# Four places of a written-out order moved: a GELU ahead of a decoding step, a join ahead of K S, a Gram ahead of two transpositions, an output on another queue

## The chip, the cores and the metric

The kernel runs on one core of a Trainium2 chip. A core has five engines, each with a queue of its own that it works through in order: TensorE (PE: matmuls, with the weight loads shown as PEld), VectorE (DVE), ScalarE (ACT), GpSimd (POOL) and SyncE (SP), which here only issues DMAs; ACT issues some too. The metric is the device time of one execution in microseconds; lower is better.

## The reference, cut to what matters

```python
# q, k, v: (4, 8, 768, 48); beta: (4, 8, 768)
k_n = k / (norm(k) + 1e-6)
for t in range(S):                       # delta rule, state of D x D for each batch and head
    y[:, :, t] = q[:, :, t] @ state
    v_old = state.T @ k_n[:, :, t]
    state = state + beta[t] * outer(k_n[:, :, t], v[:, :, t] - v_old)
x = y.transpose(0, 2, 1, 3).reshape(3072, 384)
h = x @ w_in                             # (384, 2048)
out = (0.5 * h * (1 + erf(h / sqrt(2)))) @ w_out      # (2048, 384)
```

q, k, v and beta arrive in float32; w_in and w_out arrive as float64, which the kernel reads as pairs of 32-bit words and turns into float32 itself ("decoding").

## The kernel before, in words

**Tiling.** The 768 steps are cut into 12 chunks of 64. A chunk has two units (`tiles[c, a]`, a = 0, 1), each with two batches on the two halves of the partitions and eight heads. `first`, `third` and `fourth` are the units of chunks 0 and 1, of chunk 2 and of chunk 3.

**Delta rule.** Inside a chunk the steps are solved together. Two chunks (four units) make a group g. The Gram matrices of K (`grams`, matmuls L414 by way of `products`, psum tile psG) give `G` and `diag`. VectorE eliminates the 32-wide diagonal blocks row by row in `Nu` (`eliminate_steps`, L501 and L503, one pair for a row); at the end two transpositions write the inverse to `XM` (L512) and `Zf` (L516). A "join" (`join_run`, L593, tile psJ) then builds the off-diagonal blocks: level 0 needs XM, is scaled into XM by VectorE (L605); level 1 is copied into Zf by ACT (L572). It comes in three calls, join1[0], join1[1] and join1[2], for group 1. For each chunk `against_state` multiplies K and Q with the state ("K S", L667, psK), `subtract` makes W on VectorE (L678, L684) and y on ACT (L679), `solve` gives U (psU, L702), `use` and `update` give the outputs and the state's increment (psY, L732 and L743), `outputs` writes St (L748) and x (L758), and `turn` transposes x into xT (L779, L780).

**Norms.** `norms(c)` squares K of a chunk on ACT (`ksq`), `prep(c)` sums the squares on VectorE (L349) and takes the power on GpSimd (L351), `finish(c)` makes the factors gm for the pair of chunks c and c + 1 on VectorE (L303 to L307), and the first steps of the elimination turn gm into a scaled mask (L476, L477).

**Feed-forward.** Chunks 0 and 1 use plain layers: `fc1` fills psH for a block f of 128 hidden units (three matmuls of 128x256; PE shows six, [...]and a "block" below means these six passes), ACT writes its GELU into `G` (GELU f for short); `fc2` accumulates 16 blocks into psO (L829), which ACT copies to `o_sb` and `send` writes out (L823). psH and psO have two PSUM buffers between them (tag "mlp"). Chunks 2 to 11 use a Strassen-like scheme with fewer products (`part_of_layer`, L916 and `second_layer`, L859). In its first layer a block b makes products named P1, P5, P6, P2, R22, R11, P7, P3, R12, P4, R21, in this order on PE; X1, Z1, Y1 and V1 are its psum tiles, `pu` holds copies of X1 and Z1 (ACT), L939, L968, L947 and L958 are its additions on VectorE. P4 and R21 add to Y1, so P4 must wait until L947 has read it.

**Decoding.** W_in has eight parts n; for each, `begin` isolates the exponents' bits on VectorE (L231), `exponents` turns them into float scales with two ACT instructions, `mantissas` (L251, L253) and `signed` (L261) finish the part. Part n serves blocks 2n and 2n + 1. The raw words are fetched by SP, four parts ahead. The parts of W_out follow in the same manner.

**Order.** The first part of the program is ordered by hand. The rest is a `plan`: a list of (time, step) pairs, made by `at(first, last, steps)`, which are sorted by their time and emitted (`emit`). The times are a scale of the author's, one unit for a chunk's layer, and not microseconds. VectorE runs in the emitted order; on the other engines a scheduler may shift instructions, except that `together` and `behind` chain groups of matmuls on PE, and `keep` keeps ACT instructions in the emitted order. A DMA that `fetch_in`, `load_blocks` or `send` emits stands in the issuing engine's queue and waits there until its buffer is free or its data ready.

Of the kernel before, what the change touches and what calls it, by code (L numbers as in the profile page):

```python
# [19 lines left out]
def kernel(  # L20
# [28 lines left out]
    nc = tc.nc  # L49
# [4 lines left out]
    NC = S // C  # L54
# [48 lines left out]
    for c in range(NC):  # L103
        for a in range(NA):
            u = tiles[c, a] = Unit()
# [171 lines left out]

    def decode_in():

        marks = {3: (None, 1.03, 0.99, 1.04), 4: (1.0, 1.09, 1.1, 1.13),  # L280
                 5: (1.12, 1.18, 1.14, 1.2), 6: (1.19, 1.24, 1.21, 1.25),
                 7: (1.245, 1.3, 1.29, 1.36)}
        steps = []
        for n, (a, b, c, d) in marks.items():
            if a is not None:
                steps += [(a, (begin, n))]
            steps += [(b, (exponents, n, keep)), (c, (mantissas, n)), (d, (signed, n))]
        return steps
# [349 lines left out]
    def join_steps(g):  # L638
        a, b = range(NA), range(NA, 2 * NA)
        return [(join_run, g, a, ()), (join_run, g, b, a), (join_run, g, (), b)]  # L640
# [176 lines left out]
            nc.scalar.activation(*gelu)  # L817

    def send(u, cols=slice(0, DM), queues=None):
        queues = queues or ((nc.sync, nc.sync) if 1 < u.c < NC - 1 else (nc.scalar, nc.scalar))  # L820
        for p in range(2):
            row = (2 * u.a + p) * S + u.c * C
            queues[p].dma_start(out=out[row:row + C, cols], in_=u.o[HALF[p], cols])  # L823

    def fc2(u, f0, f1):
        if f0 == 0:
            u.psO = ps.tile([128, DM], F32, tag="mlp", name="psO")
        for f in range(f0, f1):
            nc.tensor.matmul(u.psO, lhsT=G[:, u.a, f, :],  # L829
                             rhs=w_out_sb[:, f, :], start=(f == 0), stop=(f == NF - 1))  # L830
        if f1 == NF:
            u.o = wk.tile([128, DM], F32, tag="o_sb", name="o_sb")
            nc.scalar.copy(u.o, u.psO)
            send(u)
# [206 lines left out]
    def ffn_steps(c):  # L1041
        ones = [(1.3, fc1, c, f) for f in range(NF)]
        if c > 1:
            return [(0.88, part_of_layer, c, b, n) for b in range(NB)
                    for n in ("P1", "P5", "P6", "P2", "R22", "R11", "P7", "P3", "R12", "P4", "R21")] + [
                (2.6, second_layer, c, n) for n in (1, 5, 2, 6, 4, 7, 3)]
        twos = [(2.7, fc2, tiles[c, a], f, f + 4) for a in range(NA) for f in range(0, NF, 4)]
        if c == 0:
            twos.sort(key=lambda s: s[3])
            more_ = [(1.3, fc1, 1, f) for f in range(EARLY)]  # L1050
            return ones + twos[:-2 * NA] + more_[:4] + twos[-2 * NA:-NA] + more_[4:] + twos[-NA:]
        return ones[EARLY:] + twos

    def at(first, last, steps):

        total, done, timed = sum(s[0] for s in steps), 0.0, []
        for w, *step in steps:
            timed.append((first + (last - first) * (done + 0.5 * w) / total, step))
            done += w
        return timed  # L1060
# [69 lines left out]
    fourth = [tiles[3, a] for a in range(NA)]  # L1130
# [58 lines left out]
    def state_at(c, *times, first=(), second=()):  # L1189

        steps = state_steps(c, first, second)
        if len(times) > len(steps):
            steps = steps[:-1] + [(turn, tiles[c, a]) for a in range(NA)]
        return [(t, step) for t, step in zip(times, steps) if t is not None]

    plan = [at(c + 1 + 0.25 * (c == 1), c + 2 + 0.25 * (c == 0), ffn_steps(c)) for c in range(NC)]
    plan += [decode_in(), at(1.365, 1.9, decode_steps(n_in, NW)), at(1.91, 1.911, [(1.0, late)])]
    rows1, join1 = eliminate_steps(1), join_steps(1)
    plan += [at(1.06, 1.065, [(1.0, load, 3)]),
# [8 lines left out]
             at(1.455, 1.456, [(1.0, solved, first[NA + 1], kept_copy)]),  # L1208
             state_at(1, None, None, 1.5, 1.56, 1.58),
             at(1.92, 2.45, rows1[:-1]),  # L1210
             at(2.66, 2.661, [(1.0, together, join1[0])]),
             at(2.662, 2.663, rows1[-1:]),
             at(2.65, 2.651, [(1.0, sum_of_w_in, 1)]), at(2.664, 2.665, [(1.0, sum_of_w_in, 2)]), at(2.712, 2.713, [(1.0, sum_of_w_in, 4)]),
             at(2.72, 2.721, [(1.0, sum_of_w_in, 3)]),
# [25 lines left out]
    def gram(c):  # L1240
        return [(grams, [tiles[c, a] for a in range(NA)])] if c < NC else []

    def query(c):
        return [(queries, [tiles[c, a] for a in range(NA)])]

    def spread(name, n, *times):
        return [at(t, t + 0.001, [(1.0, copy_out, name, n)]) for t in times]

    def rows_of(g, w, pieces):
        rows = eliminate_steps(g)  # L1250
        assert sum(n for n, _, _ in pieces) == len(rows)
        parts, done = [], 0
        for n, first, last in pieces:
            parts += [at(w + first, w + last, rows[done:done + n])]
            done += n
        return parts
# [8 lines left out]
    for w in range(3, NC):  # L1265
        two_ahead = w + 2 < NC
        if w % 2:
            if w == 3:
                plan += [at(w + 0.09, w + 0.092, [(1.0, transposed, u, (1,)) for u in fourth]
                            + [(1.0, together, *gram(5))]),  # L1270
                         at(w, w + 0.001, [(1.0, norms, 5), (1.0, prep, 5)]),
                         at(w + 0.1, w + 0.101, [(1.0, finish, 4)])]
                plan += rows_of(2, w, ((1, 0.102, 0.103), (2, 0.16, 0.2), (4, 0.224, 0.31),
                                       (2, 0.325, 0.365), (1, 0.395, 0.4), (2, 0.485, 0.5),
                                       (2, 0.508, 0.54), (5, 0.6, 0.685), (7, 0.76, 0.88),
                                       (3, 1.0, 1.05), (5, 1.07, 1.1), (1, 1.153, 1.154),
                                       (1, 1.2, 1.201), (1, 1.201, 1.202)))
            elif two_ahead:
                plan += rows_of(w // 2 + 1, w, ((1, -0.35, -0.349), (1, -0.34, -0.339),
                                                (1, -0.23, -0.229), (5, -0.22, -0.14),  # L1280
                                                (1, -0.07, -0.06), (3, 0.005, 0.05),
                                                (3, 0.068, 0.148), (2, 0.156, 0.215),
                                                (2, 0.235, 0.31), (3, 0.325, 0.365),
                                                (1, 0.398, 0.409), (2, 0.485, 0.5),
                                                (1, 0.508, 0.54), (5, 0.6, 0.685),
                                                (3, 0.76, 0.8), (1, 1.003, 1.004),
                                                (1, 1.16, 1.161), (1, 1.166, 1.167)))
            plan += [state_at(w, w + 0.367, w + 0.59, w + 0.72, w + 0.93, second=query(w))]
        else:
            j0, j1, j2 = join_steps(w // 2)  # L1290
            t = w + (0.25 if w == 4 else 0.165)
            plan += [at(t, t + 0.001, [(1.0, together, j0, *query(w))]),
                     at(w + 0.37, w + 0.371, [(1.0, together, j1, *gram(w + 2))]),
                     state_at(w, w + 0.465, w + 0.58, w + 0.72, w + 0.93, second=[j2] + gram(w + 3))]
            plan += spread("join", 4, w + 0.395)
            plan += spread("join", 4, w + 0.64)
            if two_ahead:
                plan += spread("gram", 2, w + 0.375) + spread("gram", 2, w + 0.42)
                plan += spread("gram", 4, w + 0.63)
                plan += [at(w + 0.366, w + 0.367, [(1.0, norms, w + 2)]), at(w + 0.3715, w + 0.372, [(1.0, prep, w + 2)]),  # L1300
                         at(w + 0.56, w + 0.561, [(1.0, norms, w + 3), (1.0, prep, w + 3)]),
                         at(w + 0.64, w + 0.641, [(1.0, finish, w + 2)])]
# [32 lines left out]
```

## Time and profile before

| | |
|---|---|
| three runs | 643.37, 643.89, 644.04 us; median 643.89 |
| profiled execution | 644.36 us, of which span 642.6 us |
| PE busy | 621.4 us (97%) |
| VectorE, ACT, GpSimd busy | 496.1, 259.7, 63.7 us |
| granted TensorE clock, mean | 0.983 |
| waits of PE in the span | 2.1 us psH on ACT's G, 5.1 us psT on the first K, 3.7 us psG on Qt, 0.6 us psX on pu, 0.5 us psX on x |
| DMA | 39.79 MB, 62 GB/s |

The profile counts microseconds from the span's start. In an order of time a row gives start, length, engine, line, operation, output and inputs, count, and in brackets the idle time of the engine ahead of it with what ended it. Neighbouring rows of one engine overlap a little[...]. A row "SPq" or "ACTq" is the issue of DMAs by that queue.

### The profile page before, as it was taken

To read this page: it belongs to the slowest core of one execution; us is meant where nothing else is said; L and a number is where in the kernel's file an instruction comes from. 1 tells how busy PE (TensorE), PEld (TensorE's weight loads), DVE (VectorE), ACT (ScalarE), POOL (GpSimd) and SP (SyncE) were. 2 spreads that over 40 slices of the span, in tenths; PEclk is the share of its full clock that TensorE was granted. 3 is DMA by queue.
4 is the path that set the end of the run, shared out by engine and by line. 5 is a ranking of instruction groups with operands and counts; after the bars stand their busy time and mean duration, and the time that the engine had idled before them with its cause. 6 is when DMAs were issued, how large, how long until landed. Compare 5 with 4: busy or idle time off the path is not lost.

```text
span 642.6 us, 22154 instructions
## 1 busy us (share of the span) xinstructions
PE 621.4 (97%) x9702; PEld 575.8 (90%) x9702; DVE 496.1 (77%) x1011; ACT 259.7 (40%) x586; POOL 63.7 (10%) x58
## 2 busy tenths in 40 slices
PE   6778999999899999999999999999999999999997
PEld 5667886777699999999999999999999999999997
DVE  6999889988889997999587999587999565354342
ACT  3576776624452266132266132266132253232230
POOL 4044001100401013001013001013001000000000
PEclk9977999999999999999999999999999999999999
DMA  9895764303432335321425312311221400100100
GB/s 130 180 272 159 131 159 148 50 1 67 73 61 37 57 41 89 60 26 35 67 36 83 61 23 40 67 23 31 52 26 34 68 3 3 26 2 3 24 3 24
DMA packets 158433, 39.79 MB, mean 62 GB/s; under 512 B 150016, under 2 KB 153216, under 8 KB 158336
## 3 DMA queue, kind: packets, MB, share of 16 engines
q1 hardware_dynamic: 155344, 36.94, 29.9%
q10 hardware_dynamic: 2992, 1.43, 1.0%
q8 instruction: 76, 1.25, 0.8%
q14 instruction: 21, 0.17, 0.1%
HBM read 33.62 MB, written 4.72 MB: 60 GB/s over the span
## 4 chain that ended last, share of the span: by engine, by line
PE 86%; DVE 6%; ACT 3%; DMA 2%; issue 1%; SPq 1%; DVEq 0%; ACTq 0%
PE psX L859 12%; PE psY L916 11%; PE psX L916 8%; PE psY L859 8%; PE psH L811 6%; PE psV L916 5%; PE psO L829 5%; PE psZ L916 5%; PE psG L414 4%; PE psZ L859 4%; PE psV L859 4%; PE psK L667 3%; PE psJ L593 2%; PE psY L732 2%; PE psU L702 2%; DMA Kp<-in_k_dram 1%
## 5 line engine op out<-in xcount | busy, mean ns | idle before, releaser
L916 PE MATMUL psX<-xT,w_in_sb 128*128 128x128 f32 x480 | 64.6, 278 | 0.6 <-ACT pu L902 0.6
L503 DVE TENSOR_TENSOR Nu<-Nu,tmp 128x58 f32<-128x58 f32 (+13 forms) x168 | 58.9, 351 | 5.8
L501 DVE TENSOR_TENSOR tmp<-Nu 128x58 f32<-128x58 f32 (+13 forms) x168 | 59.0, 351 | 4.4
L916 PEld LDWEIGHTS psX<-xT,w_in_sb 128*128 128x128 f32 x480 | 58.8, 192 | 1.8 <-ACT pu L902 0.8
L902 ACT COPY xT<-psX 128x768 f32<-128x768 f32 x9 | 7.2, 798 | 124.4 <-PE psX L788 124.4
L859 PE MATMUL psX<-w_out_sb,G 128*128 128x192 f32 x320 | 55.3, 326 | 0.0
L351 POOL TENSOR_TENSOR n<-n,half 128x16 f32<-128x16 f32 x10 | 30.0, 2998 | 254.1 <-DVE n L349 194.6
L859 PEld LDWEIGHTS psX<-w_out_sb,G 128*128 128x128 f32 x320 | 52.1, 190 | 0.0
L811 PE MATMUL psH<-xT,w_in_sb 128*128 128x256 f32 x192 | 46.3, 398 | 2.2 <-ACT G L902 2.1
L811 PEld LDWEIGHTS psH<-xT,w_in_sb 128*128 128x128 f32 x192 | 37.4, 199 | 9.7 <-ACT G L902 2.7
L829 PE MATMUL psO<-w_out_sb,G 128*128 128x384 f32 x128 | 44.5, 492 | 0.0
L916 PE MATMUL psY<-xT,w_in_sb 128*128 128x128 f32 x320 | 42.3, 275 | 0.0
L902 ACT COPY pu<-psZ 128x512 f32<-128x512 f32 x40 | 23.4, 586 | 39.0 <-PE psZ L916 38.9
L916 PEld LDWEIGHTS psY<-xT,w_in_sb 128*128 128x128 f32 x320 | 38.9, 192 | 0.0
L829 PEld LDWEIGHTS psO<-w_out_sb,G 128*128 128x128 f32 x128 | 23.5, 190 | 13.6
L902 ACT ACTIVATE G<-G 128x512 f32<-128x512 f32 x40 | 25.2, 629 | 19.0 <-DVE G L947 18.3
L376 POOL TENSOR_TENSOR V<-V,n 128x384 f32<-128x384 f32 x18 | 16.2, 910 | 133.5 <-DMA V<-in_v_dram 78.4
L859 PE MATMUL psZ<-T,pu 128*128 128x192 f32 x160 | 28.6, 332 | 0.0
L859 PE MATMUL psY<-T,G 128*128 128x192 f32 x160 | 28.6, 332 | 0.0
L939 DVE TENSOR_TENSOR psY<-psY,pu 128x512 f32<-128x512 f32 x20 | 14.0, 698 | 18.7 <-PE psY L916 18.7
L859 PE MATMUL psV<-w_out_sb,G 128*128 128x192 f32 x160 | 27.7, 326 | 0.0
L859 PE MATMUL psX<-T,G 128*128 128x192 f32 x160 | 27.6, 326 | 0.0
(183 smaller groups left out, 1350.0 us busy)
## 6 DMA issues: line engine op xcount, KB each, us to landing
Kp<-in_k_dram SPq DMA_DIRECT2D x76, 96.0 KB, 3.3
w_out_sb<-in_moe_w_in_dram SPq DMA_DIRECT2D x24, 256.0 KB, 4.7
w_raw<-in_moe_w_out_dram SPq DMA_DIRECT2D x16, 384.0 KB, 4.3
V<-in_v_dram SPq DMA_DIRECT2D x48, 96.0 KB, 3.1
out_dram<-o_sb SPq DMA_DIRECT2D x36, 96.0 KB, 2.2
Qp<-in_q_dram SPq DMA_DIRECT2D x64, 32.0 KB, 2.1
Qp<-in_q_dram SPq DMA_DIRECT2D x16, 96.0 KB, 4.3
Qp<-in_k_dram SPq DMA_DIRECT2D x32, 32.0 KB, 2.5
```

The costliest lines, as they stand in the source:

```text
L351: nc.gpsimd.tensor_tensor(flat, flat, half, op=ALU.pow)
L376: engine.tensor_tensor(u.V, u.V, ns[u.c][:, u.a].unsqueeze(2).to_broadcast([128, H, D]), op=ALU.mult)
L414: nc.tensor.matmul(psG[HALF[p], r, i * NP + j, :], lhsT=u.Kt[rows, p, j, :], rhs=(u.Qt if x else u.Kt)[rows, p, j, :], start=True, stop=True)
L501: nc.vector.tensor_tensor(tmp, nu[:, j + 1:, j:j + 1].to_broadcast([128, n, j]), nu[:, j:j + 1, 0:j].to_broadcast([128, n, j]), op=ALU.mult)
L503: nc.vector.tensor_tensor(nu[:, j + 1:, 0:j], nu[:, j + 1:, 0:j], tmp, op=ALU.add)
L667: nc.tensor.matmul(u.psK[to, x, r, j, :], lhsT=(u.Qt if x else u.Kt)[rows, p, j, :], rhs=St[rows, u.a, p ^ r, j, :], start=True, stop=True)
L811: nc.tensor.matmul(psH, lhsT=w_in_sb[:, f // 2, m, f % 2 * 128:(f % 2 + 1) * 128], rhs=xTs[c][:, m, :], start=(m == 0), stop=(m == NM - 1))
L829: nc.tensor.matmul(u.psO, lhsT=G[:, u.a, f, :], rhs=w_out_sb[:, f, :], start=(f == 0), stop=(f == NF - 1))
L859: nc.tensor.matmul(ps_, lhsT=lhs[:, f, :], rhs=rhs[:, f, :], start=first and f == 0, stop=f == FH - 1, skip_group_check=not first)
L902: i = fn(*args, **kw)
L916: nc.tensor.matmul(ps_[:, i], lhsT=lhs[:, f // 2, f % 2 * 128:(f % 2 + 1) * 128], rhs=rhs, start=first and i == 0, stop=True, skip_group_c ...
L939: nc.vector.tensor_tensor(L1["Y1"], L1["Y1"], L1["pu"][:, 0], op=ALU.add)
```

## The change: four places of the order

- `decode_in`: the exponents of part 3 move from 1.03 to 1.05 and its `signed` from 1.04 to 1.06. In ACT's queue GELU 1 of chunk 0 now stands ahead of the two exponent instructions of part 3, and GELU 2 behind them; before, both stood behind. The order of the other engines is the same there.
- `plan`: the first join of group 1 moves from 2.66 to 2.595, ahead of chunk 2's K S (2.6). On PE the 16 rows of join matmuls now stand directly ahead of the 64 rows of K S, where K S and four blocks of psO stood ahead of them. The second join follows the next four psO blocks, as one piece instead of alternating with psO. On VectorE the four L605 of the first join now stand ahead of the first sum of W_in (`Sw`, L874). Seven psO blocks instead of three stand between psU and psY, and fewer earlier.
- For w = 3: the Gram of chunk 5 moves from behind Q's transpositions of chunk 3 to 3.1, ahead of them (3.19); `norms` and `prep` of chunk 5 from 3.0 to 3.06; `finish(4)` and the first elimination step by 0.01 to stay behind. On PE the Gram stands ahead of R22 and the transpositions stand between P3 and R12. On ACT the squares of chunk 5 stand behind the four copies of chunk 4's Gram, where they stood ahead of `pu`; the copies of Q's transpositions come later. On VectorE the sums of squares stand behind L939 and L968; `finish` and L477 still stand ahead of L947. GpSimd's order is the same.
- `send`: the outputs of chunk 1, two DMAs for each of its units, are issued by SP instead of ACT. SP's queue then has the first pair between V's loads and K's of chunk 5, and the second pair behind the K blocks of chunk 6 and ahead of K's of chunks 4 and 6 and Q's of chunk 4.

```diff
-        marks = {3: (None, 1.03, 0.99, 1.04), 4: (1.0, 1.09, 1.1, 1.13),
+        marks = {3: (None, 1.05, 0.99, 1.06), 4: (1.0, 1.09, 1.1, 1.13),
...
-        queues = queues or ((nc.sync, nc.sync) if 1 < u.c < NC - 1 else (nc.scalar, nc.scalar))
+        queues = queues or ((nc.sync, nc.sync) if 0 < u.c < NC - 1 else (nc.scalar, nc.scalar))
...
-             at(2.66, 2.661, [(1.0, together, join1[0])]),
+             at(2.595, 2.596, [(1.0, together, join1[0])]),
...
             if w == 3:
-                plan += [at(w + 0.09, w + 0.092, [(1.0, transposed, u, (1,)) for u in fourth]
-                            + [(1.0, together, *gram(5))]),
-                         at(w, w + 0.001, [(1.0, norms, 5), (1.0, prep, 5)]),
-                         at(w + 0.1, w + 0.101, [(1.0, finish, 4)])]
-                plan += rows_of(2, w, ((1, 0.102, 0.103), (2, 0.16, 0.2), (4, 0.224, 0.31),
+                plan += [at(w + 0.19, w + 0.191, [(1.0, transposed, u, (1,)) for u in fourth]),
+                         at(w + 0.1, w + 0.101, [(1.0, together, *gram(5))]),
+                         at(w + 0.06, w + 0.061, [(1.0, norms, 5), (1.0, prep, 5)]),
+                         at(w + 0.11, w + 0.111, [(1.0, finish, 4)])]
+                plan += rows_of(2, w, ((1, 0.112, 0.113), (2, 0.16, 0.2), (4, 0.224, 0.31),
```

## The prediction

> **What bounds the kernel now.** I read the page first, then the waits of PE, then the order of instructions around each of the three edited places, and the granted clock there. On the page, PE is busy for 97% of the span, and the chain that ended last lies on PE for 86%.
>
> ```profile
> PE 621.4 (97%) x9702; PEld 575.8 (90%) x9702; DVE 496.1 (77%) x1011; ACT 259.7 (40%) x586; POOL 63.7 (10%) x58
> ```
>
> So time can only be won where PE stands still or runs slowly. The waits of PE (engine, line, releaser: sum, times, longest):
>
> ```profile
> PE psH L811 <- ACT G L902: 2.1, 1, 2.1
> ...
> PE psX L916 <- ACT pu L902: 0.6, 1, 0.6
> PE psX L779 <- DVE x L758: 0.5, 1, 0.5
> ```
>
> The first is one stall of 2.1 us in chunk 0's first layer; the others lie at the two later edits. A fourth, psG on Qt, is 1.0 us of the 3.7 that its line sums. ACT's order of time shows why the first exists:
>
> ```profile
> 57.95 0.39 ACT L902 ACTIVATE G<-psH 128x256 f32<-128x256 f32 x1 [1.79 <-PE psH L811]
> 61.31 2.13 ACT L902 ACTIVATE w_e<-w_e,lim 128x768 f32<-128x768 int32 x2 [2.97 <-DVE w_e L231]
> 63.31 0.61 ACT L902 ACTIVATE G<-psH 128x256 f32<-128x256 f32 x2
> ```
>
> ACT is idle for 2.97 us while GELU 1's input is ready from about 59.4 (block 0 ended at 57.95; six more passes, 12 in 2.86 us at 73.57); it stands behind the exponents of W_in's group 3, which wait for VectorE. psH has two buffers, so block 3 cannot start before GELU 1. The clock around it (stretch: length, PE busy, granted clock, DMA):
>
> ```profile
> 26.23:29.65 3.42, 2.37 (x37) 1.00 0.60 108
> ...
> 60.37:63.78 3.41, 1.34 (x66) 1.00 0.86 268
> 63.78:67.19 3.41, 3.41 (x8) 0.50 1.04 280
> ```
>
> A window with 1.34 us of PE work is followed by one at half clock, one with 2.37 is not. The stall therefore costs twice.
>
> Place B is the join of group 1; VectorE and PE there:
>
> ```profile
> 137.79 2.08 DVE L512 STREAM_TRANSPOSE XM<-Nu 128x1024 f32<-128x1024 f32 x1
> ...
> 141.60 1.20 DVE L874 TENSOR_TENSOR Sw<-w_in_sb 128x1024 f32<-128x1024 f32 x1
> ```
>
> XM ends at 139.87; PE starts K S at 139.44, and the join only at 144.22. PE is busy for 27.36 of the 27.90 us from 139.5 to 167.4. Place C is chunk 2's first block, where ACT is last:
>
> ```profile
> 167.50 0.48 ACT L833 COPY o_sb<-psO 128x384 f32<-128x384 f32 x1 [1.46 <-DMA Qp<-in_k_dram]
> 168.01 2.46 ACTq L823 DMA_DIRECT2D out_dram<-o_sb  x2
> 170.59 0.94 ACT L902 ACTIVATE ksq<-Kp 128x384 f32<-128x384 f32 x2 [2.61 <-DMA Kp<-in_k_dram]
> 171.43 0.56 ACT L902 COPY pu<-psX 128x512 f32<-128x512 f32 x1
> ...
> 172.24 2.90 POOL L351 TENSOR_TENSOR n<-n,half 128x16 f32<-128x16 f32 x1 [7.45 <-DMA out_dram<-o_sb]
> ...
> 177.43 1.22 DVE L477 TENSOR_TENSOR XM<-low,gt 128x1024 f32<-128x1024 f32 x1
> ...
> 179.62 0.69 DVE L947 TENSOR_TENSOR G<-psY,pu 128x512 f32<-128x512 f32 x1 [0.96 <-ACT pu L902]
> ```
>
> The two sends and the squares of chunk 5 hold pu back. The last three lines become important below.
>
> [...]L307 takes 0.75 us beside GpSimd's V scaling and 0.19 at 112.27 without.
>
> **A, exponents behind GELU 1.** Nothing is added. GELU 1 runs at about 59.4 in ACT's idle time. Block 3 then starts when the join's first level ends (60.43 + 1.20 = 61.63), instead of 63.70. Six passes at full clock take 1.43 (12 in 2.86 at 73.57): to 63.06. Block 4 needs GELU 2, still behind the exponents (61.31 + 2.13 = 63.44, then 0.25): 63.70. PE idles 0.64 in the window instead of 2.07, less than the 1.05 of the harmless one, so I take full clock: block 4 ends at 65.13, not 68.24. Next is the join's second level, which waits for L559 on VectorE (64.46 + 1.41 = 65.87): 65.95 instead of 68.25, a gain of 2.3. Were the clock still half, block 4 would end at 65.97 and half the join be slow: gain 1.6. What follows moves along: group 5's exponents come after GELU 5, and VectorE, idle for 2.60 us before 73.33 and released by exactly these exponents, moves too, and again at 88.83 and 89.77, where PE's psY releases it after 1.17 and 0.38. The raw W_in that VectorE then wants 2.3 us earlier, at 73.4 instead of 75.70, was issued by 64.62 and lands in 4.7 (the page's DMA issues): hidden. SP's 16 loads from 73.59 end at 83.54 and then precede the fetch issued at 84.76; up to 1 us of it may stay, against some 3 us of slack to its use at 93.56. From 89.77 to 142.8 VectorE has hardly a pause, so both engines reach B 2.3 us earlier. Everything below is in the old clock, without these 2.3.
>
> **B, join ahead of K S.** Same instructions. PE is free at 139.51 and must wait for XM: 139.93, a new 0.42 of idling. VectorE's join products then come directly after Zf (141.73 to 143.5), not at 145.42, and Sw 1, which covered it, moves behind. W, y, U and x come about 2 us earlier; seven instead of three second-layer passes stand ahead of psY, so PE, not VectorE, sets x, and the waits on x (0.5) go. PE's idle sum was 27.90 − 27.36 = 0.54; it becomes about 0.42 and I take −0.2 with the pieces of joins that no longer alternate with psO. Bounds: −0.5 (all of it) and +0.4 (the wait alone).
>
> **C, sends, squares and Gram 5.** The 2.46 us of sends leave ACT, so pu follows psX at once and the 0.6 goes; Gram 5 takes a free PSUM buffer instead of one under Q's transposition, so the 1.0 goes. PE's work up to P4 (psY<-TX) is 11.97 us: it could reach P4 at 167.4 + 11.97 = 179.4 instead of 181.0. But the squares now stand behind Gram 4's four copies on ACT. Gram 4 starts at 169.18; its copies start 1.22 later (175.40 to 176.62 for the other Gram): 170.40; the four take 2.35 (176.62 to 178.97): 172.75. Before, from the squares' start to the end of L477 it was 178.65 − 170.59 = 8.06 (squares, sums, power on GpSimd 2.90, factors, gm, XM); that gives 180.81. L947 is queued behind L477 on VectorE and takes 0.69: 181.5, and P4 waits for it. So P4 comes 0.5 later than before, after a stall of 181.5 − 179.4 = 2.1. VectorE itself is 1.2 late at L482; 0.31 of idling at 189.34 takes some back, and at the next XM (227.78 + 0.9) it meets PE's join (228.08 + 0.5), without more loss. Bounds of C: −1.6 (stall hidden) to +2.2 (half clock after it: 3.41 us at half speed lose 1.7).
> On SP the sends stand before other things. The first pair precedes K 5's four loads, which then end by about 159 and land in 3.3, wanted at 172.75. The second pair waits for o_sb at 168.0 and has behind it Kp 4, K 6 and the 16 Q loads; these also wait for Q's transposition, some 5 us later now: 178.6 + 9.0 = 187.6, against L404 at 216.23. Without these covers each us would count; here I cost them at nothing.
>
> **Sum.** −2.3 − 0.2 + 0.5 = −2.0. The profiled execution took 644.36 (span 642.6 and 1.8 around it): 642.4. The median of the three runs, 643.89, is 0.5 below it: 641.9 is the forecast.
>
> **Rivals.**
> The clock falls at C: the 2.1 us stall looks like the 2.07 of A. For it: the same length[...]. Against: in A the rest of the window was joins on 32-row tiles, at C it is full-array products[...]. Price 1.7: −0.3, so 643.6.
> Slower: VectorE's elimination does not move with A. Place: the join at 139.87. PE then arrives 2.3 earlier and waits 2.7, A's gain is gone, and such a wait brings half clock, 1.7: 0 − 0.2 + 0.5 + 1.7 = +1.8, so 645.7. For it: VectorE hardly pauses for 53 us before; against: the pauses at 73.33, 88.83 and 89.77 tie its start to ACT and PE. It decides if XM moves by less than about 0.7.
> The stall at C is partly covered: L306 and L307 miss the V scaling (1.34 becomes 0.38), the power is read sooner. −3.0, so 640.9. For it: the overlap depends on GpSimd's timing; against: GpSimd still runs both in the same order.
> That the edits do nothing is excluded: the orders of ACT, PE, VectorE and SP differ in the built program.
>
> **How the numbers follow.** Forecast 0.50, clock at C 0.26, slower 0.15, better 0.09. A measurement here tells about 0.2%, 1.3 us, from nothing: faster is below 642.6, slower above 645.2. Each case has an error of about 0.8 us. Faster: most of the forecast (0.42), the better one (0.09) and a little of the clock case (0.03): 0.54. Slower: most of the slower case and a tail: 0.15. The rest, 0.31, is the same. The likeliest case alone spans 640.8 to 643.0. From 640.3 to 645.1 leaves out the worst of the slow and of the better case.
>
> **What would show it.** A: the wait of psH on G near 0.6, no half clock from 63 to 67, XM's L512 at 135.5. B: psJ directly before psK and a wait of 0.4 on XM; no wait on x. C: no sends in ACT's queue at 165; squares after the fourth copy; a wait of psY<-TX on L947 of about 2 us; the clock after it. I am wrong if XM has not moved, if that wait is absent or above 3 us, or if a new wait on DMA appears.

## The result, and the profile after

The changed kernel takes 645.96 us (median of 20 runs, 644.79 to 647.30) against 643.51 us before (20 runs, 641.38 to 645.42). The ratio is 1.0039 with a 95% interval of 1.0028 to 1.0050: 2.5 us slower, where the forecast said 641.9 and gave "slower" 0.15. The profiled execution after took 644.96 us, with a span of 643.2. That is only 0.6 us over the profiled execution of before, because one lies 1.0 below its kernel's median and the other 0.85 above. The profiles therefore tell where time moves, the medians how much.

First the page of the changed kernel, busy time by engine, and then its waits of PE (engine, line, releaser: sum, times, longest).

```profile
PE 617.9 (96%) x9702; PEld 573.8 (89%) x9702; DVE 496.3 (77%) x1011; ACT 259.9 (40%) x586; POOL 66.0 (10%) x58
```

```profile
PE psY L916 <- DVE G L947: 4.0, 1, 4.0
PE psG L414 <- ACT Qt L394: 2.7, 4, 0.7
...
PE psJ L548 <- DVE XM L559: 2.0, 2, 1.5
...
PE psJ L593 <- DVE XM L512: 0.5, 1, 0.5
PE psH L811 <- ACT G L902: 0.4, 1, 0.4
```

The old waits at A and C (psH 2.1, psX on pu 0.6, psG's longest of 1.0) and the one on x are gone or small. One wait of 4.0 us, which the kernel before did not have, is now the second largest of all. GpSimd's busy time has grown by 2.3 us although it has the same 58 instructions; 1.45 us of that is a single instruction, which place C shows.

**Place A.** ScalarE in order of time, changed kernel (start, duration, instruction, in brackets the idle time before it and what ended it):

```profile
59.64 0.39 ACT L902 ACTIVATE G<-psH 128x256 f32<-128x256 f32 x1 [0.91 <-PE psH L811]
61.50 2.14 ACT L902 ACTIVATE w_e<-w_e,lim 128x768 f32<-128x768 int32 x2 [1.47 <-DVE w_e L231]
```

GELU 1 now runs in the pause, and the exponents start at 61.50, about where they did before (61.31). Block 3 of psH starts at 61.96 instead of 63.70. VectorE moves along: L748 starts at 86.79 instead of 88.83, 2.04 earlier, and XM of group 1 (next fence, VectorE in order of time at B) starts at 135.71 instead of 137.79, 2.08 earlier.

```profile
135.71 2.09 DVE L512 STREAM_TRANSPOSE XM<-Nu 128x1024 f32<-128x1024 f32 x1
137.70 1.93 DVE L516 STREAM_TRANSPOSE Zf<-Nu 128x1024 f32<-128x1024 f32 x1
139.66 1.74 DVE L605 TENSOR_TENSOR XM<-psJ,gm 32x256 f32<-32x256 f32 x4
141.43 1.22 DVE L874 TENSOR_TENSOR Sw<-w_in_sb 128x1024 f32<-128x1024 f32 x1
```

**Place B.** The join's products (L605) follow Zf directly and Sw comes behind them. Chunk 2's first pass on PE (the kernel before, then the changed one) starts 2.94 us earlier, and 0.9 of them are won at B:

```profile
167.30 1.05 PE L916 MATMUL psX<-xT,w_in_sb 128*128 128x128 f32 x8
164.36 1.05 PE L916 MATMUL psX<-xT,w_in_sb 128*128 128x128 f32 x8
```

Hardly any of this 0.9 is idle time. From the end of the psO blocks ahead of K S and the join to chunk 2's first pass, PE idles for 0.54 us before (139.50 to 167.30) and 0.48 after (137.47 to 164.36), but it is busy for 26.41 us instead of 27.26 with the same matmuls (567 records before, 566 after). The second join alternates with psO before and runs as one piece after.

**Place C.** More than that is lost again here. The next fences are ScalarE, VectorE and GpSimd of the changed kernel in order of time.

```profile
164.56 0.48 ACT L833 COPY o_sb<-psO 128x384 f32<-128x384 f32 x1 [1.46 <-PE psO L829]
165.45 0.59 ACT L902 COPY pu<-psX 128x512 f32<-128x512 f32 x1 [0.41 <-PE psX L916]
...
169.84 0.94 ACT L902 ACTIVATE ksq<-Kp 128x384 f32<-128x384 f32 x2
```

```profile
170.40 1.01 DVE L349 TENSOR_REDUCE n<-ksq 128x8 f32<-128x384 f32 x2 [0.30 <-ACT ksq L902]
171.33 1.75 DVE L842 TENSOR_TENSOR T<-w_out_sb,T 128x1536 f32<-128x1536 f32 x1
175.87 0.18 DVE L303 TENSOR_SCALAR n<-n 128x32 f32<-128x32 f32 x1 [2.79 <-POOL n L351]
...
178.13 1.23 DVE L477 TENSOR_TENSOR XM<-low,gt 128x1024 f32<-128x1024 f32 x1
179.27 0.68 DVE L947 TENSOR_TENSOR G<-psY,pu 128x512 f32<-128x512 f32 x1
```

```profile
171.49 4.35 POOL L351 TENSOR_TENSOR n<-n,half 128x16 f32<-128x16 f32 x1 [10.76 <-DMA Kp<-in_k_dram]
```

The sends have left ScalarE, pu follows o_sb at once, and the squares come at 169.84, after Gram 4's copies. The power starts at 171.49, when the sums (L349) have just ended at 171.41; its bracket names a load of K that landed about then. On GpSimd it takes 4.35 us instead of the 2.90 of before: it starts 0.16 us after VectorE's product T and ends 2.8 us after that product does. VectorE stands idle for 2.79 us until the power is there; then come the factors, L477, and only then L947. PE waits for it, as its order of time and its stretches (length, PE busy, granted clock, DMA share, GB/s) show:

```profile
180.01 1.56 PE L916 MATMUL psY<-TX,w_in_sb 128*128 128x128 f32 x8 [4.00 <-DVE G L947]
181.36 1.91 PE L916 MATMUL psY<-xT,w_in_sb 128*128 128x128 f32 x8
183.07 1.51 PE L916 MATMUL psX<-xT,w_in_sb 128*128 128x128 f32 x8
184.42 1.06 PE L916 MATMUL psZ<-TX,Sw 128*128 128x128 f32 x8
```

```profile
60.37:63.78 3.41, 3.15 (x73) 1.00 0.81 264
63.78:67.19 3.41, 2.80 (x70) 1.00 0.97 266
...
177.19:180.61 3.42, 0.60 (x5) 1.00 0.43 50
180.61:184.02 3.41, 3.41 (x18) 0.50 0.38 45
```

The kernel before, for comparison:

```profile
180.83 1.06 PE L916 MATMUL psY<-TX,w_in_sb 128*128 128x128 f32 x8
...
183.51 1.06 PE L916 MATMUL psZ<-TX,Sw 128*128 128x128 f32 x8
```

At A the clock is full where it had been half. It is half at C instead: the 24 matmuls from 180.01 to 184.42 need 4.41 us, where the same 24 needed 2.68 before (180.83 to 183.51). So the balance at psZ is −2.94 from A and B, +2.12 for the later P4 and +1.73 for the clock, together +0.91. Up to the end of the span 0.3 of that comes back.

### The profile page after: what moved, and what is told of

The parts are those of the page before. It is cut to its first block, busy times and chain, and to the rows that moved or that the text cites. A ratio compares the mean times of both kernels' runs of the same rounds, so it can differ in the third digit from the quotient of the medians.

```text
span 643.2 us, 22156 instructions
## 1 busy us (share of the span) xinstructions
PE 617.9 (96%) x9702; PEld 573.8 (89%) x9702; DVE 496.3 (77%) x1011; ACT 259.9 (40%) x586; POOL 66.0 (10%) x58
## 3 DMA queue, kind: packets, MB, share of 16 engines
q10 hardware_dynamic: 2672, 1.03, 0.8%
## 4 chain that ended last, share of the span: by engine, by line
PE 77%; DVE 14%; DMA 2%; issue 2%; SPq 2%; ACT 1%; POOL 1%; DVEq 0%; POOLq 0%
PE psX L859 12%; PE psY L916 11%; PE psY L859 8%; PE psX L916 8%; PE psV L916 5%; PE psZ L916 5%; PE psZ L859 4%; PE psV L859 4%; PE psK L667 3%; DVE Nu L503 3%; DVE tmp L501 3%; PE psG L414 3%; PE psJ L593 3%; PE psH L811 2%; PE psY L732 2%
## 5 line engine op out<-in xcount | busy, mean ns | idle before, releaser
L351 POOL TENSOR_TENSOR n<-n,half 128x16 f32<-128x16 f32 x10 | 31.4, 3145 | 251.8 <-DVE n L349 191.2
L939 DVE TENSOR_TENSOR psY<-psY,pu 128x512 f32<-128x512 f32 x20 | 14.0, 698 | 22.4 <-PE psY L916 19.6
```

What stands on the lines that cost most here:

```text
L351: nc.gpsimd.tensor_tensor(flat, flat, half, op=ALU.pow)
```

## The experiments

Each edit stands against the kernel named; each ratio is to the kernel before. That kernel was timed again beside each group of runs: its median was 644.03 us beside the first four, 643.52 beside the next four and 644.44 beside the last two.

### Which part loses: A, B and C alone, and all but C's new order

A alone, against the kernel before:

```diff
-        marks = {3: (None, 1.03, 0.99, 1.04), ...
+        marks = {3: (None, 1.05, 0.99, 1.06), ...
```

> Only the marks of W_in's part 3 are changed (exponents behind GELU 1). Theory: A is sound and its gain lasts to the end by itself: psH's wait on G falls from 2.1 to about 0.5, no half clock at 63 to 67, XM of group 1 (L512) near 135.8, the end 2.0 us earlier than the profiled execution of before, so a median near 641.5. Rival: A's gain exists only in executions[...]; then the median of many runs gains clearly less, about 1 us or none (642.5 to 643.5). A second rival, that what A gains is waited for at the join of group 1, gives a wait on XM of 2 us or more and no gain.

641.84 us (22 runs), ratio 0.9969 (0.9958 to 0.9980): 2.0 us faster. The clock is full at 63 to 67, psH waits 0.9, and all of the gain reaches the end. No wait of 2 us appears at the join of group 1. The theory holds, both rivals fall.

B alone, against the kernel before:

```diff
-             at(2.66, 2.661, [(1.0, together, join1[0])]),
+             at(2.595, 2.596, [(1.0, together, join1[0])]),
```

> Only the join of group 1 is put ahead of K S. Theory: B gains 0.9 us by itself (the changed kernel showed 2.94 us at chunk 2's first pass, of which A had 2.08): wait on XM about 0.4, no wait on x, chunk 2's first pass 0.9 earlier, median near 642.6. Rival: the 0.9 came with A's earlier start (other timing of DMA and GpSimd around it); then B alone gives 0.2 or nothing, 643.3 or more.

643.79 us (14 runs), ratio 0.9999 (0.9980 to 1.0017): this can't tell a gain of 0.9 from none. The trace shows the exchange of waits, 0.5 on XM in place of 0.5 on x, and the stretch from the join on about 0.8 shorter (0.34 later at psY at 158.41, 0.50 earlier at the second psX, 165.01). The trace shows what the theory said, the median lies where the rival put it, and the interval allows both.

C alone (sends on SyncE and the new order of chunk 2's first block), against the kernel before:

```diff
-        queues = queues or ((nc.sync, nc.sync) if 1 < u.c < NC - 1 else (nc.scalar, nc.scalar))
+        queues = queues or ((nc.sync, nc.sync) if 0 < u.c < NC - 1 else (nc.scalar, nc.scalar))
...
-                plan += [at(w + 0.09, w + 0.092, [(1.0, transposed, u, (1,)) for u in fourth]
-                            + [(1.0, together, *gram(5))]),
-                         at(w, w + 0.001, [(1.0, norms, 5), (1.0, prep, 5)]),
-                         at(w + 0.1, w + 0.101, [(1.0, finish, 4)])]
+                plan += [at(w + 0.19, w + 0.191, [(1.0, transposed, u, (1,)) for u in fourth]),
+                         at(w + 0.1, w + 0.101, [(1.0, together, *gram(5))]),
+                         at(w + 0.06, w + 0.061, [(1.0, norms, 5), (1.0, prep, 5)]),
+                         at(w + 0.11, w + 0.111, [(1.0, finish, 4)])]
...
```

> Only the sends on SyncE and the new order in chunk 2's first block (squares behind the Gram copies, Gram 5 ahead of Q's transpositions). Theory: C alone costs 3.5 to 4: wait of psY<-TX on L947 about 4.0, GpSimd's power 4.35 instead of 2.90 because VectorE's T product starts just ahead of it, a half-clock window of 3.41 behind the wait, median near 647. Rival: the wait is the price of A and B, which bring PE forward but not the chain VectorE to GpSimd; then the wait here is about 1 us, full clock follows, and the median is near 643.5.

649.62 us (6 runs), ratio 1.0096 (1.0069 to 1.0122). The wait is the whole one; here is the waits view of C alone:

```profile
PE psY L916 <- DVE G L947: 4.0, 1, 4.0
```

So it isn't that A and B brought PE forward past its partners: the chain over ScalarE, VectorE and GpSimd moved along with them, and the wait belongs to C. In the trace C costs 3.7 us from 158 to 189 us (2.16 late against before's trace, then 5.88; the rest is start-up). The ratio's interval says 4.4 to 7.9, more than the 3.5 to 4 expected; six runs don't settle the difference.

A, B and the sends, with chunk 2's first block in its old order, against the changed kernel:

```diff
-                plan += [at(w + 0.19, w + 0.191, [(1.0, transposed, u, (1,)) for u in fourth]),
-                         at(w + 0.1, w + 0.101, [(1.0, together, *gram(5))]),
-                         at(w + 0.06, w + 0.061, [(1.0, norms, 5), (1.0, prep, 5)]),
-                         at(w + 0.11, w + 0.111, [(1.0, finish, 4)])]
+                plan += [at(w + 0.09, w + 0.092, [(1.0, transposed, u, (1,)) for u in fourth]
+                            + [(1.0, together, *gram(5))]),
+                         at(w, w + 0.001, [(1.0, norms, 5), (1.0, prep, 5)]),
+                         at(w + 0.1, w + 0.101, [(1.0, finish, 4)])]
...
```

> A, B and the sends on SyncE, with chunk 2's first block in its old order. Theory: all the loss lies in that order: no wait on L947, the gains of A and B and of the sends (pu no longer behind them, 0.6) reach the end: 3 to 3.5 us, median near 640.3. Rival: the sends on SyncE delay the loads of Q, K and V behind them; then new waits on DMA appear in chunk 2 and the median stays above 642.

640.14 us (10 runs), ratio 0.9946 (0.9929 to 0.9963): 3.5 us faster than before. No wait on L947, no new wait on DMA, PE reaches P4 at 176.55 without a pause (PE in order of time, A, B and the sends):

```profile
176.55 1.06 PE L916 MATMUL psY<-TX,w_in_sb 128*128 128x128 f32 x8
```

From chunk 2's first pass (164.98) to P4 it needs 11.57 us, the changed kernel 11.65 without its wait. The new place of Gram 5 has therefore nothing left to win once the sends are off ScalarE.

### Which edit of C: the squares or the Gram

Squares back at their old place, against the changed kernel:

```diff
-                         at(w + 0.06, w + 0.061, [(1.0, norms, 5), (1.0, prep, 5)]),
+                         at(w, w + 0.001, [(1.0, norms, 5), (1.0, prep, 5)]),
```

> The changed kernel with the squares of chunk 5 back at their old place, ahead of pu (Gram 5 stays ahead of Q's transpositions, the sends stay on SyncE). Theory: the late squares alone make the loss; L947 ends near 176.4, as in the kernel with A, B and the sends, P4 waits less than 0.3, no half clock behind it, median 640.2. Rival: the Gram's move matters too (Q's transpositions late, two half copies of Qt apart); then 642 or more, with a wait on Qt or L947.

640.20 us (6 runs), ratio 0.9944 (0.9923 to 0.9966). ScalarE and then GpSimd of this kernel in order of time:

```profile
165.19 0.48 ACT L833 COPY o_sb<-psO 128x384 f32<-128x384 f32 x1 [1.46 <-PE psO L829]
165.56 0.94 ACT L902 ACTIVATE ksq<-Kp 128x384 f32<-128x384 f32 x2
```

```profile
167.45 2.90 POOL L351 TENSOR_TENSOR n<-n,half 128x16 f32<-128x16 f32 x1 [6.10 <-DVE n L349]
```

The squares use the time in which the sends used to sit and delay pu by nothing that PE notices. The power is over at 170.35, before T starts at 170.63. L947 ends at 176.37 and P4 starts at 176.47.

The reverse, Gram 5 back at its old place and the squares late, against the changed kernel:

```diff
-                plan += [at(w + 0.19, w + 0.191, [(1.0, transposed, u, (1,)) for u in fourth]),
-                         at(w + 0.1, w + 0.101, [(1.0, together, *gram(5))]),
+                plan += [at(w + 0.09, w + 0.092, [(1.0, transposed, u, (1,)) for u in fourth]
+                            + [(1.0, together, *gram(5))]),
```

> The changed kernel with Gram 5 back behind Q's transpositions, squares still behind Gram 4's copies. Theory: the loss stays whole, because the chain from the squares to L947 is the same: wait of P4 on L947 about 4.0, power 4.35, half clock behind it, median near 646. Rival: half of the loss is the Gram's; then the wait is near 2 and the median near 643.

646.06 us (13 runs), ratio 1.0044 (1.0030 to 1.0058): as slow as the changed kernel. Its waits view, and GpSimd:

```profile
PE psY L916 <- DVE G L947: 3.8, 1, 3.8
```

```profile
171.66 4.34 POOL L351 TENSOR_TENSOR n<-n,half 128x16 f32<-128x16 f32 x1 [10.76 <-DMA Kp<-in_k_dram]
```

The two runs together settle it: with early squares the place of the Gram makes no difference (640.14 and 640.20), with late squares neither (646.06 and 645.96). The ratios say the same (0.9946 and 0.9944, 1.0044 and 1.0039). The squares' place is worth some 5.8 us in the medians, and the traces have the same 5.8: from chunk 2's first pass to psZ it takes 20.06 us in the changed kernel (164.36 to 184.42) and 14.23 with early squares (164.99 to 179.22).

### What the late squares cost: the power, the queue, the clock

VectorE's product T ahead of L939, so that it runs in a pause and not beside the power, against the changed kernel:

```diff
-at(3.07, 3.071, [(1.0, sum_of_w, 4)])
+at(2.962, 2.963, [(1.0, sum_of_w, 4)])
```

> The changed kernel with VectorE's product T (L842, 1.75 us) moved ahead into VectorE's pause before L939, so that none of it runs beside GpSimd's power. Theory: the power lasts 2.90 again instead of 4.35, L947 ends 1.45 earlier, P4 waits 2.5 instead of 4.0, XM of group 2 comes 1.45 earlier; the half clock behind the wait stays, since 2.5 is more than the 2.07 of A: gain 1.45, median near 644.5; were the clock full, 642.8. Rival: the power is long for another reason (its input, DMA writing into SBUF); then 4.35 and the wait of 4.0 stay, and the median is near 646.

643.97 us (14 runs), ratio 0.9997 (0.9981 to 1.0012), 2.0 below the changed kernel's median. VectorE, GpSimd, and PE's order and stretches of this kernel:

```profile
166.06 1.75 DVE L842 TENSOR_TENSOR T<-w_out_sb,T 128x1536 f32<-128x1536 f32 x1
170.71 1.01 DVE L349 TENSOR_REDUCE n<-ksq 128x8 f32<-128x384 f32 x2 [0.31 <-ACT ksq L902]
```

```profile
171.80 2.90 POOL L351 TENSOR_TENSOR n<-n,half 128x16 f32<-128x16 f32 x1 [10.76 <-DVE n L349]
```

```profile
178.88 2.07 PE L916 MATMUL psY<-TX,w_in_sb 128*128 128x128 f32 x8 [2.56 <-DVE G L947]
```

```profile
175.35:178.76 3.41, 0.97 (x9) 1.00 0.47 69
178.76:182.18 3.42, 3.30 (x15) 0.50 0.42 50
```

One instruction of VectorE in another place, and the power is 2.90 again and the wait 1.44 shorter. So T was what lengthened the power. The half clock stays: the same 24 matmuls take 4.34 us (178.88 to 183.22), 1.66 more than at full clock. From chunk 2's first pass (164.67) to psZ the trace has 18.55 us instead of 20.06, a gain of 1.5 as expected; that the median gains 2.0 and lies 0.5 under the expected 644.5 stays open.

The factors queued behind L947, against the changed kernel:

```diff
-                         at(w + 0.11, w + 0.111, [(1.0, finish, 4)])]
-                plan += rows_of(2, w, ((1, 0.112, 0.113), (2, 0.16, 0.2), ...
+                         at(w + 0.17, w + 0.171, [(1.0, finish, 4)])]
+                plan += rows_of(2, w, ((1, 0.172, 0.173), (2, 0.174, 0.2), ...
```

> The changed kernel with the factors of chunk 5 and the first step of group 2's elimination (L303 to L477) queued on VectorE behind L947 instead of ahead of it. Theory: L947 needs none of them and runs near 174, P4 does not wait and keeps full clock; but the elimination of group 2 starts only 0.6 us earlier than in the changed kernel, so PE comes about 5 us earlier to the join of group 2 and waits there 3 to 4 us on XM (L512), perhaps with half clock after it: the stall moves, and the median is 644 to 646. Rival: VectorE has slack enough in the 48 us of the elimination; then XM comes earlier too, and the median is near 640.5.

644.95 us (14 runs), ratio 1.0016 (1.0000 to 1.0032). VectorE, ScalarE and PE of this kernel, in order of time:

```profile
174.05 0.69 DVE L947 TENSOR_TENSOR G<-psY,pu 128x512 f32<-128x512 f32 x1 [0.58 <-ACT pu L902]
176.25 0.18 DVE L303 TENSOR_SCALAR n<-n 128x32 f32<-128x32 f32 x1 [1.52 <-POOL n L351]
...
182.82 0.68 DVE L958 TENSOR_TENSOR G<-psV,pu 128x512 f32<-128x512 f32 x1
```

```profile
183.59 0.59 ACT L902 COPY pu<-psZ 128x512 f32<-128x512 f32 x1 [3.83 <-DVE G L958]
```

```profile
176.24 1.06 PE L916 MATMUL psY<-TX,w_in_sb 128*128 128x128 f32 x8
...
184.23 1.16 PE L916 MATMUL psZ<-xT,w_in_sb 128*128 128x128 f32 x8 [2.47 <-ACT pu L902]
```

P4 does not wait: L947 needs nothing of the factors, it only stood behind them. That the stall would move was right, the place was wrong. It isn't at the join of group 2 but 8 us on: pu's copy of psZ waits for its buffer, which L958 frees, and L958 stands behind the factors and the first steps of the elimination. Behind this pause of 2.47 us (181.76 to 184.23) the clock stays full. One difference to the other pauses is an estimate: in the changed kernel's trace the clock changes at 44.08, 57.73, 180.61 and 184.02 us, and these lie 4, 36 and 1 times 3.413 us apart. In the trace of this run full clock begins at 56.83. Counted on from there in the same steps, 183.12 (37 steps) falls within the pause; no change of the clock shows there. The two stretches beside it:

```profile
179.71:183.12 3.41, 2.05 (x19) 1.00 0.43 50
183.12:186.54 3.42, 2.31 (x92) 1.00 0.14 19
```

Each holds at least 2.05 us of PE work. In the 3.41 us ahead of the half clock there were 0.97 with T early and 0.60 in the changed kernel.

### B and the sends on top of A

A and the sends, against the kernel before:

```diff
-        marks = {3: (None, 1.03, 0.99, 1.04), ...
+        marks = {3: (None, 1.05, 0.99, 1.06), ...
...
-        queues = queues or ((nc.sync, nc.sync) if 1 < u.c < NC - 1 else (nc.scalar, nc.scalar))
+        queues = queues or ((nc.sync, nc.sync) if 0 < u.c < NC - 1 else (nc.scalar, nc.scalar))
```

> A and the sends on SyncE, without B. Theory: the sends on ScalarE held pu and, through the copies of Qt, Gram 5; off that queue psX no longer waits for pu and psG waits less for Qt: 0.8 to 1 us on top of A, median near 640.9 against 641.8 of A alone; the wait on x (0.5) stays. Rival: ScalarE has slack there once A has moved it (A alone already showed no wait of psX on pu), so the sends are worth 0.3 or less: 641.5 or more.

640.88 us (6 runs), ratio 0.9951 (0.9932 to 0.9969). psG's waits on Qt fall to 2.7 in all, 0.7 at most, as in the changed kernel; the wait of 0.5 on x stays.

A and B, against the kernel before:

```diff
-        marks = {3: (None, 1.03, 0.99, 1.04), ...
+        marks = {3: (None, 1.05, 0.99, 1.06), ...
...
-             at(2.66, 2.661, [(1.0, together, join1[0])]),
+             at(2.595, 2.596, [(1.0, together, join1[0])]),
```

> A and B, with the sends of chunk 1 on ScalarE as before. Theory: B is worth 0.7 to 0.9 us: the wait on x goes, one of 0.5 on XM comes, and the pieces of the join no longer alternate with psO; median near 641.0. Rival: B only exchanges one wait of 0.5 for another; then 641.5 or more.

641.06 us (9 runs), ratio 0.9952 (0.9938 to 0.9967). psG's longest wait on Qt is 1.0 again, psX waits 0.4 for pu, and the wait on x is gone. Both agree with the theory (640.9 and 641.0), but their intervals overlap with that of A alone, so that B and the sends are each worth something like 0.8 us by the traces (the sends: 6.13 us from chunk 2's first pass to Gram 5, instead of 6.88 with A alone; B: 0.8 in B alone, 0.9 in the changed kernel) and not by the medians alone.

The lowest medians of all are those of A, B and the sends with the squares early, 640.1 to 640.2 us with Gram 5 in either place; their intervals overlap with those of the last two kernels.

## Why the prediction was wrong

**A was right**, in mechanism and size: −2.3 predicted, −2.04 in the trace of the changed kernel and −2.0 in the median of A alone. The clock stayed full, the join's second level waited for L559 as foreseen, and VectorE moved (L512 foreseen at 135.5, found at 135.71). Of the 0.3 too much, 0.07 is a reading: the trace of before has the join's second level at 68.18, not 68.25. Since VectorE moved, the rival of the slower side, that the elimination would not move, falls, although the kernel did get slower. That the rival's 645.7 lies so near the measured 645.96 is chance: the wait of 2.7 that it foresaw at the join did not come (0.5 was measured). Its sum also has a slip, since 0 − 0.2 + 0.5 + 1.7 is +2.0, not +1.8.

**B was under-sized**: −0.2 predicted, −0.9 in the trace. The wait of 0.5 on XM came and that on x went, as said; but the sum counted only PE's idle time of 0.54 and gave −0.5 as the most that B could win. The gain came from PE's busy time, 26.41 us instead of 27.26. That the second join in one piece is what shortens it is argued and not shown: no run moves it without the first join.

**C is the step that failed**: "P4 comes 0.5 later than before": P4 came 2.12 later, and with the half clock behind it the step cost 3.85. That is 3.35 more than foreseen: 1.45 for GpSimd's power, 0.17 because the prediction put the old P4 at 181.0 where its trace has 180.83, and 1.73 for the clock. The chain was named rightly and in the right order: the squares were worked out for 172.75 in the old clock, that is 169.81 with the 2.94 won, and came at 169.84. Three terms of its working were off.

- "from the squares' start to the end of L477 it was 178.65 − 170.59 = 8.06" took GpSimd's power at 2.90 from a place where it starts 1.24 us ahead of the product T (VectorE, the kernel before; the power starts at 172.24):

```profile
173.48 1.75 DVE L842 TENSOR_TENSOR T<-w_out_sb,T 128x1536 f32<-128x1536 f32 x1
```

In the new order VectorE's queue has T directly behind the sums L349, so T starts first, and the power took 4.35. That is +1.45, shown by moving T alone. The prediction had a like case in L307, 0.75 us beside GpSimd's V scaling and 0.19 without it, but it did not look at what stands beside the power in the new order. The trace of the kernel before already held a power behind a product, at 51.24 (VectorE, then GpSimd):

```profile
50.62 1.47 DVE L253 SCALAR_TENSOR_TENSOR w_in_sb<-w_out_sb,w_in_sb 128x768 f32<-128x768 uint32 x1
51.24 3.85 POOL L351 TENSOR_TENSOR n<-n,half 128x16 f32<-128x16 f32 x1
```

The product starts 0.62 us ahead, and the power takes 0.95 longer than its usual 2.90.

- "it could reach P4 at 167.4 + 11.97 = 179.4" was 0.4 late: PE needs 11.65 from chunk 2's first pass to P4, not 11.97. This made the stall longer, not the end later.
- The clock was left out of the sum and kept as a rival at 1.7 and chance 0.26. It cost 1.73. The longer stall alone does not account for that: the kernel with T early has a stall of 2.56 and also fell to half clock.

The prediction had written that it would be wrong if that wait were above 3 us; it was 4.0. It had also costed the sends on SyncE at nothing for DMA, and no run showed a new wait of PE on DMA. What it did not ask is whether C's order was needed at all: the gains of 0.6 and 1.0 credited to C (pu, and Gram 5's wait) are the sends' work, and with the sends alone moved they come without the chain to L947.

The counterpart that stays unexplained: the profiles of before and after differ by 0.6 us, the medians by 2.5. Single executions of the kernel before range over 5 us (39 executions, 641.0 to 646.7), those of the kernel with A, B, the sends and the old order over 2.5 (10 executions), those with the squares moved back over 1.0 (6 executions). It fits that a stall costs a half-clock stretch in some executions and not in others, as the pauses of 2.56 and 2.47 us did, but no run separates this from other differences of start-up.

## What to carry to other kernels

When an instruction is moved later, follow its result through every queue to PE, and redo each duration on the way with the neighbours that it will have in the new order; a duration from the old place need not hold beside the new neighbours (the power: 2.90 us there, 4.35 here). The old trace may hold the price of the new ones elsewhere, as with the power of 3.85 us here. In an in-order queue, ask what unrelated work stands behind the step that will now be waited for: here L947 needed nothing of the factors ahead of it, and started at 174.05 ahead of them, at 179.27 behind them. And where one edit (the sends) already frees the engine, test it without the reordering that seems to belong with it.

## What the runs showed of the hardware

GpSimd's power on 128x16 takes 2.90 us (the median of ten in the kernel before). It takes about as long when one of two products of VectorE starts behind it, and the product is not slowed either: in the kernel before, T starts 1.24 us behind a power (2.90 for the power, and 1.75 for T, which takes 1.75 in its early place too, with GpSimd idle), and L261 0.10 us behind another (2.94 for the power at 107.12, 0.97 for L261, which takes 0.96 at 63.47 with GpSimd idle). It takes longer when the product starts ahead of it: 4.35 us with T 0.16 us ahead, 3.85 with L253 0.62 us ahead. The extra 1.45 and 0.95 are close to what was left of the product when the power started (1.59 and 0.85). What makes the order of the two starts count was not shown.

For the clock, pauses of PE of 2.07, 2.56 and 4.00 us were each followed by one stretch of 3.41 us at half clock, and one of 2.47 us was not. So in these traces the length of a pause alone does not decide. In the 3.41 us ahead of the half clock stood 1.34, 0.97 and 0.60 us of PE work; the two stretches that share the pause of 2.47 us hold 2.05 and 2.31. That the place of a pause counts is an estimate from the steps of 3.413 us between the changes of the clock in the changed kernel's trace (57.73 to 180.61 is 36 of them). How much work keeps the clock full does not follow from busy time alone: in the kernel before, 46.72 to 50.13 us holds 2.56 us of PE work, most of it on 64x64 tiles and at half clock, and half clock goes on to 56.95 all the same.
